# A fused Nystrom attention and feed-forward kernel: smaller first weight chunks, the sums of q of batch 0 on GpSimd, and v loaded in gated pieces

## Chip, cores and metric

The kernel runs on one core of a Trainium2 chip. The metric is the device time of one execution in microseconds (us); of several executions the median is given. The engines are called PE (TensorE's matmuls), DVE (VectorE), ACT (ScalarE), POOL (GpSimd) and SP (SyncE, which only issues DMAs).

## What is computed

Attention by landmarks for 8 batches of 8 heads, 576 tokens and 64 features; then a feed-forward part without nonlinearity. Cut to what matters:

```python
q_lm = q.reshape(B, H, 32, 18, 64).mean(axis=3)        # k_lm likewise
A, Bm, C = sm(q, k_lm), sm(q_lm, k_lm), sm(q_lm, k)    # softmax of scaled products
Z = Bm.T / (norm1(Bm) * norminf(Bm) + 1e-6)
for _ in range(6):
    Z = 2 * Z - Z @ Bm @ Z
x = heads_side_by_side(A @ Z @ C @ v)                  # 4608 x 512
out = (((x @ w1) * (x @ w2)) @ w3) @ w_out             # w1, w2: 512x1024; w3: 1024x1024; w_out: 1024x512
```

## The kernel before

Since nothing stands between w3 and w_out, the kernel first folds them into one 1024x512 matrix (`w34`), once; this is the *fold*. Then it runs batch after batch. For a batch, `attention` (L178) computes landmark scores, the iterated inverse and the small matrices `g` (L403) and `ahat` (L355); the *up* stage (`up`, L422) makes from them, for each of 8 slices of 128 hidden features, two products of 128x576, which ACT copies (`a_sb`, L430) and DVE multiplies (`ab`, L432); the *down* stage (`down`, L439) multiplies `ab` by `w34`, and SP writes the rows out.

**The order is written out by hand.** The schedule is manual: each engine executes its instructions in the order in which the Python code emits them, and a wait at the head of an engine's queue holds all that is behind it. `attention` and `fold` are generators; `steps(g, n)` (L517) runs n pieces of one, and this is how attention of the next batch is woven into the matmuls of the present one. The attention generator has 18 pieces: the landmarks' transposition (L183, first use of `parts`), the small score matrix, two score pieces, and so on, up to four pieces that make `g`.

**The fold** (`fold`, L464). w_out and w3 are float32 and are split into a high and a low float16 term, and a product of two split blocks takes three matmuls (L490): high-high, high-low and low-high. `split(i)` does this for w_out, two row chunks of 128 at a time, both terms on DVE (L469 the high term, L471 the low one). `turn(j, cc)` transposes four 128x128 blocks of w3 on PE (L477); ACT makes their high term (L482) and DVE their low one (L483). `product(j, c)` multiplies them. 64 products are made, in the order of `order` (L499); the dict `before` (L496) says which splits and turns are emitted ahead of which product. Ahead of all this stand 10 matmuls on a zeroed tile (`warm`, L546 to L550), which compute nothing that is used.

**Loads of the fold.** SP loads w3 (first two blocks in halves of 256 KB, L538 to L544), ACT's queue loads w_out in pieces of 512 KB (`load_wout`, L533). GpSimd's queue loads q and k (`load_qk`, L68, float32 in memory to float16) and w1, w2 (`load_weight`, L80). So that these do not crowd the first weights, GpSimd first does a tiny copy from w_out's second piece (`gate`, L552). Two more such gates let w3(4) wait for k of batch 0 (L565) and v of batch 0 for its q (L571).

**The landmarks.** k and q are needed with features on the partitions (`qkT`). For batch 0 PE transposes them (`turn_on_pe`, L94, copies by ACT and DVE, L104), for the others DMA transposes on SP do it (`transposes`, L85, four for a batch in `turn_all`, L512). `landmarks` (L158) sums each 18 tokens: six operations (L166 to L175) for each of k (t=1) and q (t=0), which leave a high and a low term in `parts`. Every such sum is on GpSimd, save that of q of batch 0, which is on DVE (L577), in two halves of 4 heads.

**Around the main loop.** attention of batch 0 runs among the later products of the fold (L581 to L595); in the loop over batches (L600), batch b's up and down stages carry attention of b+1. At the top of batch b SP gets the transposes and the load of v (1152 KB) for b+2 (L604, L605). Behind the up stage GpSimd gets the loads of q and k for b+3 and the landmarks of b+2 (L616 to L619). In the up stage one piece of attention goes into each slice; batch 0 differs (L613: none in the first two, two in the last, and two at a time later in the down stage).

Of the kernel before, what the change touches and what calls it, by code (L numbers as in the profile page):

```python
# [31 lines left out]
def kernel(  # L32
# [46 lines left out]

    def load_weight(t, w):  # L80
# [77 lines left out]
    def landmarks(st, t, eng=nc.gpsimd):  # L158
        if "parts" not in st:
            st["parts"] = pz.tile([128, 2, 2, H, 32], FP16, name="parts")  # L160
        for h0 in ((0,) if eng is nc.gpsimd else (0, 4)):
# [5 lines left out]
            eng.tensor_tensor(out=tr, in0=tr, in1=x[:, :, 2, :], op=ALU.add)  # L167
            t3 = tr.rearrange("p h (l g) -> p h l g", g=3)
# [4 lines left out]

            eng.tensor_copy(out=hi, in_=o)
            eng.tensor_tensor(out=lo, in0=o, in1=hi, op=ALU.subtract)  # L175

# [287 lines left out]
    def fold(pf, wof, w3f, wsp):  # L464
        turned, psW = {}, {}

        def split(i):
            sl = slice(2 * i, 2 * i + 2)
            nc.vector.tensor_scalar(out=wsp[:, 0, sl, :], in0=wof[i], scalar1=WS, scalar2=None,  # L469
                                    op0=ALU.mult)  # L470
            nc.vector.scalar_tensor_tensor(out=wsp[:, 1, sl, :], in0=wof[i], scalar=WS,  # L471
                                           in1=wsp[:, 0, sl, :], op0=ALU.mult, op1=ALU.subtract)
# [13 lines left out]
        def product(j, c):  # L486
# [5 lines left out]
            if c == 7:  # L492
# [3 lines left out]
        before = {0: [(turn, 0, 0), (split, 0), (turn, 1, 0), (split, 1)],  # L496
                  2: [(turn, 0, 1)], 3: [(split, 2)], 6: [(turn, 1, 1)], 7: [(split, 3)],
# [25 lines left out]
    with tc.tile_pool(name="pf", bufs=2) as pf:  # L523
# [3 lines left out]
        def load_w3(j, cc=None):  # L527
            if j not in w3f:
                w3f[j] = pf.tile([128, DF], FP32, name="w3f", bufs=3)
            sl = slice(0, DF) if cc is None else slice(512 * cc, 512 * cc + 512)  # L530
            nc.sync.dma_start(out=w3f[j][:, sl], in_=moe_w3[128 * j:128 * (j + 1), sl])

        def load_wout(i, eng):  # L533
            wof[i] = pf.tile([128, 2, DM], FP32, name="wof", bufs=3)
            eng.dma_start(out=wof[i],
                          in_=moe_w_out[256 * i:256 * i + 256, :].rearrange("(c p) f -> p c f", p=128))
# [3 lines left out]
        load_w3(1, 0)  # L540
        load_wout(1, nc.scalar)
        load_w3(0, 1)
        load_wout(2, nc.scalar)
        load_w3(1, 1)  # L544

# [3 lines left out]
        for _ in range(10):  # L549
            nc.tensor.matmul(psw[:, 0, :], warm[:, 0:128], warm, start=True, stop=True)  # L550

        nc.gpsimd.tensor_copy(out=gate, in_=wof[1][:, 0, 0:1])  # L552
        load_qk(sts[0], 0)
        load_weight(0, moe_w1)
        load_weight(1, moe_w2)
        mask4, par, ones, eye2, iit, onesq, selc, lomask = constants()
        fd = fold(pf, wof, w3f, wsp)
# [102 lines left out]
```

The softmax here doesn't subtract the row's maximum and nothing guards it: scores larger than these inputs give would overflow.

## Time and profile before

| | us |
|---|---|
| median of 8 runs | 296.65 |
| lowest and highest | 294.14, 298.13 |
| the profiled execution | 294.14 |
| its span, first to last instruction | 292.1 |
| PE, DVE, ACT, POOL busy | 274.4, 173.8, 123.7, 141.3 |
| fold with attention of batch 0 (0 to 75.8) | 75.8 |
| batches 0 to 6 of the loop (75.8 to 270.0) | 194.2 |
| batch 7 (270.0 to the end) | 22.1 |

How to read the views: the page's slices cut the span into 40 equal parts of 7.3 us, and a digit is the busy share in tenths; PEclk is the clock granted to TensorE, in the same way. A table by stages gives for stretches of the span the busy time of PE, of its weight loads (PEld), of DVE, ACT and POOL, each with the number of instructions, then the granted clock, the busy share of the DMA engines and the GB/s. A timeline lists instructions in order of time: start, duration, engine, line, operation, what it writes and reads, and in brackets how long the engine was idle before it and what ended that. The chain is what the end is traced back through: start, duration, engine and line. A busy PE is a modelled figure, since matmuls overlap: six matmuls of 512 columns in a row take 1.29 us, one alone shows 0.38.

### The profile page before, as it was taken

How to read it: one execution, taken by the hardware profiler on the slowest of the kernel's cores; microseconds unless marked ns; L12 is line 12 of the kernel's file. 1: busy time of each engine (PE TensorE's matmuls, PEld its weight loads, DVE VectorE, ACT ScalarE, POOL GpSimd, SP SyncE). 2: the span in 40 equal slices, each digit the busy share in tenths (PEclk: the TensorE clock that was granted, in tenths of full speed). 3: DMA queues.
4: the chain of work that ended last, by engine and by line, in shares of the span. 5: the costliest groups of instructions: out<-in, count | busy, mean ns of one | idle time of the engine just before them, and what ended most of it. 6: DMA issues, size and time to landing. Idle time of an engine off the chain costs nothing.

```text
span 292.1 us, 9448 instructions
## 1 busy us (share of the span) xinstructions
PE 274.4 (94%) x4026; PEld 151.1 (52%) x4026; DVE 173.8 (60%) x442; ACT 123.7 (42%) x199; POOL 141.3 (48%) x184
## 2 busy tenths in 40 slices
PE   6899699999999899999999999999999999999993
PEld 3456346443674367436644754375457435744641
DVE  8943743375375676647656766477576656665720
ACT  3134135033471375147426723572466246625531
POOL 1608106295069839923991697069819921500000
PEclk9999889999999999999999999999999999999999
DMA  7999999919948579938996999399968532012124
GB/s 240 288 240 244 236 272 274 170 17 198 196 83 131 145 135 203 214 108 120 183 217 165 159 210 197 90 162 223 207 124 169 119 93 74 2 38 75 37 66 113
DMA packets 61385, 45.56 MB, mean 156 GB/s; under 512 B 34976, under 2 KB 53408, under 8 KB 61344
## 3 DMA queue, kind: packets, MB, share of 16 engines
q1 hardware_dynamic: 46896, 31.86, 48.8%
q0 software_dynamic: 13632, 11.54, 25.2%
q10 hardware_dynamic: 816, 1.57, 1.5%
q8 instruction: 31, 0.51, 0.7%
q14 instruction: 10, 0.08, 0.1%
HBM read 38.80 MB, written 9.44 MB: 165 GB/s over the span
## 4 chain that ended last, share of the span: by engine, by line
PE 80%; DVE 10%; ACT 6%; issue 2%; DVEq 0%; ACTq 0%
PE big L426 18%; PE acc L446 13%; PE acc L490 12%; PE big L446 11%; PE big L412 6%; DVE ab L432 4%; PE big L369 4%; ACT a_sb L430 3%; PE small L305 2%; PE big L477 2%; PE acc L305 2%; PE small L490 2%; PE big L224 2%; PE big L353 1%; PE big L274 1%
## 5 line engine op out<-in xcount | busy, mean ns | idle before, releaser
L426 PE MATMUL big<-ahat,gt 128*128 128x288 f16 x512 | 74.1, 286 | 2.5 <-ACT a_sb L430 1.7
L432 DVE TENSOR_TENSOR ab<-a_sb,big 128x576 f16<-128x576 f16 x64 | 48.0, 750 | 19.6 <-PE big L426 8.4
L426 PEld LDWEIGHTS <-gt 128*128 128x128 f16 x512 | 47.2, 98 | 19.0 <-issue 4.1
L430 ACT CAST a_sb<-big 128x576 f16<-128x576 f32 x64 | 40.9, 639 | 36.7 <-PE big L426 35.9
L235 POOL TENSOR_TENSOR t<-ect 96x384 f32<-96x384 f32 x16 | 15.9, 994 | 78.4 <-ACT ect L228 77.7
L490 PE MATMUL acc<-wsp,w3t 128*128 128x512 f16 x168 | 42.6, 388 | 5.1 <-DVE w3t L483 2.7
L446 PE MATMUL acc<-w,ab 128*128 128x512 f16 (+1 forms) x192 | 41.0, 382 | 0.1
L446 PEld LDWEIGHTS <-ab 128*128 128x128 f16 (+1 forms) x320 | 24.0, 100 | 32.7 <-issue 9.8
L446 PE MATMUL big<-w,ab 128*128 128x512 f16 x128 | 32.8, 381 | 0.3 <-DVE ahat L356 0.3
L490 PEld LDWEIGHTS <-w3t 128*128 128x128 f16 x192 | 18.1, 99 | 25.0 <-issue 5.5
L418 DVE TENSOR_SCALAR gt<-big 128x1024 f16<-128x1024 f32 x16 | 19.6, 1225 | 17.9 <-PE big L412 17.9
L166 POOL TENSOR_TENSOR tr<-qkT 128x768 f32<-128x768 f16 x15 | 24.6, 1641 | 10.8 <-DMA qkT<-qkn 7.1
L452 ACT ACTIVATE o_sb<-acc 128x512 f32<-128x512 f32 x20 | 11.9, 597 | 38.5 <-PE acc L446 37.6
L167 POOL TENSOR_TENSOR tr<-tr,qkT 128x768 f32<-128x768 f32 x15 | 24.6, 1641 | 1.2
L483 DVE SCALAR_TENSOR_TENSOR w3t<-big,w3t 128x512 f16<-128x512 f32 x16 | 11.0, 690 | 16.7 <-ACT w3t L482 16.7
L416 ACT ACTIVATE gt<-big 128x1024 f16<-128x1024 f32 x16 | 16.4, 1023 | 7.9 <-PE big L412 7.9
L482 ACT ACTIVATE w3t<-big 128x512 f16<-128x512 f32 x16 | 9.5, 596 | 23.2 <-PE big L477 18.3
L412 PE MATMUL big<-wup,zt 64*32 64x512 f16 x512 | 19.3, 381 | 0.0
L452 ACT ACTIVATE o_sb<-big 128x512 f32<-128x512 f32 x16 | 9.6, 597 | 21.6 <-PE big L446 21.6
L228 ACT ACTIVATE ect<-big 96x768 f32<-96x768 f32 x16 | 12.9, 806 | 3.3 <-PE big L224 2.9
L356 DVE TENSOR_TENSOR ahat<-eat,big 128x576 f16<-128x576 f16 x16 | 11.9, 749 | 1.2 <-PE big L353 1.2
L172 POOL TENSOR_TENSOR o<-o,tr 128x256 f32<-128x256 f32 x15 | 12.0, 799 | 1.2
(313 smaller groups left out, 354.5 us busy)
## 6 DMA issues: line engine op xcount, KB each, us to landing
vt<-in_v_dram SPq DMA_DIRECT2D x8, 1152.0 KB, 8.9
qkn<-in_k_dram POOLq DMA_DIRECT2D x8, 576.0 KB, 10.1
qkn<-in_q_dram POOLq DMA_DIRECT2D x8, 576.0 KB, 12.4
out_dram<-o_sb SPq DMA_DIRECT2D x24, 192.0 KB, 2.3
w3f<-in_moe_w_dram SPq DMA_DIRECT2D x6, 512.0 KB, 8.2
out_dram<-o_sb SPq DMA_DIRECT2D x24, 128.0 KB, 2.3
wup<-in_moe_w_dram POOLq DMA_DIRECT2D x4, 512.0 KB, 19.4
wof<-in_moe_w_out_dram ACTq DMA_DIRECT2D x3, 512.0 KB, 7.5
```

The lines of the kernel that those rows point to most:

```text
L166: eng.tensor_tensor(out=tr, in0=x[:, :, 0, :], in1=x[:, :, 1, :], op=ALU.add)
L167: eng.tensor_tensor(out=tr, in0=tr, in1=x[:, :, 2, :], op=ALU.add)
L235: nc.gpsimd.tensor_tensor(out=t3[0:NP], in0=e[:, :, 0:3, :], in1=e[:, :, 3:6, :], op=ALU.add)
L412: nc.tensor.matmul(psG[32 * h:32 * h + 32, qd, :], zt[rs, i, h, :], wup[rs, h, w, fs], start=(i == 0), stop=(i == 1), tile_position=(64 * ...
L416: nc.scalar.activation(out=g[:, :, w, fs], in_=psG, func=AXF.Copy, scale=1.0 / ZS)
L418: nc.vector.tensor_scalar(out=g[:, :, w, fs], in0=psG, scalar1=1.0 / ZS, scalar2=None, op0=ALU.mult)
L426: nc.tensor.matmul(p[:, c, 0:HS], st["g"][:, qd, w, 128 * j:128 * j + 128], st["ahat"][qd][:, c, :], start=(qd == 0), stop=(qd == 1))
L430: nc.scalar.copy(out=st["a_sb"], in_=p[:, :, 0:HS])
L432: nc.vector.tensor_tensor(out=st["ab"][:, j, :].rearrange("p (c s) -> p c s", c=2), in0=st["a_sb"], in1=p[:, :, 0:HS], op=ALU.mult)
L446: nc.tensor.matmul(pso[o:o + sz, :], ab[:, j, s0:s0 + sz], w34[:, j, :], start=(j == 0), stop=(j == 7), tile_position=(0, o))
L452: nc.scalar.activation(out=o_sb, in_=pso[:, :], func=AXF.Copy, scale=1.0 / (X64 * X64))
L490: nc.tensor.matmul(psW[j][:, :], turned[j, c // 4][:, a, c % 4, :], wsp[:, b, c, :], start=(c == 0 and a + b == 0), stop=(c == 7 and a == 1))
```

## The change

- w_out is loaded in eight chunks of 128 rows (256 KB) instead of four pieces of two; the first six are shared out between SP's and ACT's queues, beside the first halves of w3, of which one goes to ACT's queue. `split` works on one chunk, with the high term on ACT. The gate of GpSimd's loads is on chunk 4.
- Of the matmuls on zeros 7 stand ahead instead of 10; 3 come behind the first turn and 2 behind the second. The splits and turns are emitted at other products.
- q and k of batch 1 are loaded right behind those of batch 0, ahead of w1 and w2. v of batch 0 and its gate are emitted ahead of the landmarks of k. q of batch 0 is turned after 5 instead of 8 products behind k, and its landmarks are on GpSimd. w3(6) and the DMA transposes of batch 1 are emitted ahead of attention of batch 0, w3(7) with v of batch 1 and the landmarks of batch 1 earlier within it. Ahead of the loop one piece of attention of batch 1 is emitted.
- In the loop, v of b+2 comes in four pieces of two heads at slices 4 to 7 of the up stage. Ahead of each, ACT copies one column of `a_sb` into the piece's place; so the DMA waits for that copy. The landmarks of b+2 are emitted behind slice 5, and q and k of b+3 in four pieces among their operations. Batch 0 gets one piece of attention in each slice, as the others.

```diff
+    def load_v_piece(st, b, i, done):
+        if i == 0:
+            st["vt"] = pin.tile([128, H, 384], FP32, name="vt")
+        hs = slice(2 * i, 2 * i + 2)
+        nc.scalar.copy(out=st["vt"][0:NP, 2 * i, 0:1], in_=done)
+        nc.sync.dma_start(out=st["vt"][0:NP, hs],
+                          in_=v[b, hs].rearrange("h (p r) d -> p h (r d)", p=NP))
+
+    def qk_pieces(st, b):
+        st["qkn"] = pin.tile([128, 2, H, 384], FP16, name="qkn")
+        for t, src in ((1, k), (0, q)):
+            for i in range(2):
+                hs = slice(4 * i, 4 * i + 4)
+                nc.gpsimd.dma_start(out=st["qkn"][0:NP, t, hs, :],
+                                    in_=src[b, hs].rearrange("h (p r) d -> p h (r d)", p=NP))
+                yield
...
-    def landmarks(st, t, eng=nc.gpsimd):
+    def landmarks(st, t, eng=nc.gpsimd, pieces=iter(())):
...
             eng.tensor_tensor(out=tr, in0=tr, in1=x[:, :, 2, :], op=ALU.add)
+            next(pieces, None)
...
             eng.tensor_tensor(out=lo, in0=o, in1=hi, op=ALU.subtract)
+            next(pieces, None)
...
-        def split(i):
-            sl = slice(2 * i, 2 * i + 2)
-            nc.vector.tensor_scalar(out=wsp[:, 0, sl, :], in0=wof[i], scalar1=WS, scalar2=None,
-                                    op0=ALU.mult)
-            nc.vector.scalar_tensor_tensor(out=wsp[:, 1, sl, :], in0=wof[i], scalar=WS,
-                                           in1=wsp[:, 0, sl, :], op0=ALU.mult, op1=ALU.subtract)
+        def split(c):
+            hi, lo = wsp[:, 0, c, :], wsp[:, 1, c, :]
+            nc.scalar.activation(out=hi, in_=wof[c], func=AXF.Copy, scale=WS)
+            nc.vector.scalar_tensor_tensor(out=lo, in0=wof[c], scalar=WS, in1=hi,
+                                           op0=ALU.mult, op1=ALU.subtract)
...
-        before = {0: [(turn, 0, 0), (split, 0), (turn, 1, 0), (split, 1)],
-                  2: [(turn, 0, 1)], 3: [(split, 2)], 6: [(turn, 1, 1)], 7: [(split, 3)],
+        before = {0: [(split, 0), (turn, 0, 0), (warm_up, 3), (split, 1), (turn, 1, 0), (warm_up, 2)],
+                  2: [(split, 2)], 3: [(split, 3)], 5: [(turn, 0, 1)], 6: [(split, 4)],
+                  7: [(split, 5), (turn, 1, 1)], 10: [(split, 6)], 11: [(split, 7)],
                   14: [(turn, 2, 0)]}
...
         load_w3(0, 0)
         load_wout(0, nc.scalar)
-        load_w3(1, 0)
-        load_wout(1, nc.scalar)
+        load_wout(1, nc.sync)
+        load_w3(1, 0, nc.scalar)
+        load_wout(2, nc.sync)
+        load_wout(3, nc.scalar)
         load_w3(0, 1)
-        load_wout(2, nc.scalar)
+        load_wout(4, nc.scalar)
         load_w3(1, 1)
+        load_wout(5, nc.scalar)
...
-        nc.gpsimd.tensor_copy(out=gate, in_=wof[1][:, 0, 0:1])
+        nc.gpsimd.tensor_copy(out=gate, in_=wof[4][:, 0:1])
         load_qk(sts[0], 0)
+        load_qk(sts[1], 1)
         load_weight(0, moe_w1)
...
         load_w3(4)
+        sts[0]["vt"] = pin.tile([128, H, 384], FP32, name="vt")
+        nc.gpsimd.tensor_copy(out=sts[0]["vt"][0:NP, 0, 0:1], in_=sts[0]["qkn"][0:NP, 0, 0, 0:1])
+        load_v(sts[0], 0)
         turn_on_pe(sts[0], 1, 0, nc.scalar.copy)
         turn_on_pe(sts[0], 1, 4, nc.vector.tensor_copy)
         landmarks(sts[0], 1)
-        sts[0]["vt"] = pin.tile([128, H, 384], FP32, name="vt")
-        nc.gpsimd.tensor_copy(out=sts[0]["vt"][0:NP, 0, 0:1], in_=sts[0]["qkn"][0:NP, 0, 0, 0:1])
-        load_v(sts[0], 0)
-        load_qk(sts[1], 1)
-        steps(fd, 8)
+        steps(fd, 5)
         turn_on_pe(sts[0], 0, 0, nc.scalar.copy)
         turn_on_pe(sts[0], 0, 4, nc.vector.tensor_copy)
-        landmarks(sts[0], 0, nc.vector)
-        steps(fd, 3)
+        landmarks(sts[0], 0)
         load_w3(5)
         steps(fd, 4)
+        load_w3(6)
+        turn_all(1)
+        steps(fd, 6)
         at = attention(sts[0])
...
         if b + 2 < B:
             turn_all(b + 2)
-            load_v(sts[b + 2], b + 2)
...
-            steps(at, (0, 0, 1, 1, 1, 1, 1, 2)[j] if b == 0 else 1)
+            steps(at, 1)
+            if b + 2 < B and j > 3:
+                load_v_piece(sts[b + 2], b + 2, j - 4, st["a_sb"][0:NP, 0, 0:1])
             up(st, j, 1)
-        if b + 3 < B:
-            load_qk(sts[b + 3], b + 3)
-        if b + 2 < B:
-            landmarks(sts[b + 2], 1)
-            landmarks(sts[b + 2], 0)
+            if b + 2 < B and j == 5:
+                pieces = qk_pieces(sts[b + 3], b + 3) if b + 3 < B else iter(())
+                landmarks(sts[b + 2], 1, pieces=pieces)
+                landmarks(sts[b + 2], 0, pieces=pieces)
```

## The prediction

> **What bounds the kernel now.** I read the page's busy time and slices first, then stage tables, then the timelines of the stages with idle TensorE.
>
> ```profile
> PE 274.4 (94%) x4026; PEld 151.1 (52%) x4026; DVE 173.8 (60%) x442; ACT 123.7 (42%) x199; POOL 141.3 (48%) x184
> ...
> PE   6899699999999899999999999999999999999993
> ...
> PEclk9999889999999999999999999999999999999999
> ```
>
> PE sets the time: 274.4 of 292.1 us. It is idle for 17.7 us, and it ran slow in the fifth and sixth slice (29 to 44 us). The table by stages says where (first number the stretch's length, second PE's busy time, PEclk near the end):
>
> ```profile
> 32.00:35.00 3.00, 0.27 (x3) 0.05 (x1) 2.72 (x7) 0.00 (x0) 0.00 (x0) 0.97 1.12 246
> 35.00:38.50 3.50, 3.50 (x11) 1.85 (x12) 0.69 (x1) 0.60 (x1) 0.00 (x0) 0.54 1.18 259
> ...
> 75.80:103.40 27.60, 26.18 (x457) 14.67 (x455) 16.94 (x45) 13.24 (x22) 17.82 (x22) 1.00 0.65 128
> ...
> 132.10:158.80 26.70, 26.01 (x458) 14.86 (x457) 17.31 (x46) 13.35 (x22) 17.79 (x22) 1.00 0.98 175
> ...
> 243.50:270.00 26.50, 25.80 (x458) 14.84 (x457) 17.22 (x45) 13.20 (x22) 4.77 (x8) 1.00 0.15 42
> ```
>
> A batch of the main loop leaves PE idle 0.7 us. Batch 6 (243.5), with hardly any DMA or GpSimd work beside it, is only 0.2 us shorter than batch 2 (132.1): nothing done to the loads there can win more than about 0.2 us a batch. The loss is in the fold, and it has two places. The hole at 32 us, in the chain that ended last:
>
> ```profile
> 28.78 0.76 DVE qkT L104
> 29.54 0.47 DVE trv L166
> ...
> 34.00 0.29 DVE parts L175
> 34.30 0.61 DVE w3t L483
> 34.91 0.05 issue
> 34.95 0.61 PE acc L490
> ```
>
> The sums of q (L166 to L175) stand on VectorE ahead of w3t's low term, which PE needs. PE waits 2.73 us, then runs at clock 0.54. The other place is the start, on PE's timeline:
>
> ```profile
> 6.14 0.66 PE L477 MATMUL big<-ident,w3f 128*128 128x128 f32 x4 [0.77 <-DMA w3f<-in_moe_w_dram]
> 7.75 0.38 PE L490 MATMUL acc<-wsp,w3t 128*128 128x512 f16 x1 [0.95 <-DVE wsp L469]
> 9.02 1.24 PE L490 MATMUL acc<-wsp,w3t 128*128 128x512 f16 x5 [0.88 <-DVE wsp L471]
> ```
>
> [...] 0.54 after 2.73 us of idling; 0.95 us did not do it. [...] k and then q of batch 0, issued at 8.95 and 9.90, landed after 9.8 and 11.8 us, in order, with the weights of SP between them. [...]
>
> **The start, part by part.** Removed: VectorE's high terms (0.68 us for two row chunks) and the wait for 512 KB pieces. Added: eight ScalarE high terms, two dummies more in all, and five DMAs on ScalarE's queue instead of three. Before, the first 256 KB of w3 landed 3.5 us after 0.74, at 4.24, beside half of w_out's first piece; w3's second wait ended at 6.14 (about 1 MB moved), the gate on w_out's second piece at 8.81 (about 2 MB). That is 2.67 us per MB, so pairs of 256 KB land at about 4.3, 5.6, 7.0, 8.3, 9.7. ScalarE issues at 0.49 us each; in the compiled order its fifth DMA also waits for w_out chunk 0 (4.3), and the table load (1.28 us in the trace) stands behind it: 4.3 + 0.49 + 1.28 = 6.1. Then ScalarE works every 0.5 us (0.60 each, overlapping, as at 18.93 and 19.43[...]): chunk 0 done at 6.7, w3t 7.2, chunk 1 7.7, w3t 8.2. VectorE is free of the constants at 6.50; its low terms at about 0.65 us (half of 1.23; w3t 0.69) end at 7.35, 7.95, 8.5, 9.1, 9.7, 10.3. At 0.215 us a matmul PE then issues the first four products by 8.2, 8.9, 9.6 and 10.2, and with two more and one turn (0.43) it stands at 11.95. Before, it stood behind the same six and that turn at 13.12, where the next turn started. Gain 1.2 us; nothing if ScalarE came 1.2 later, 1.6 if it needed no wait for chunk 0. The dummies cost nothing: they fill the waits for w3 and for the terms (4.9 to 7.2). Later splits add 0.6 us on a ScalarE that idled 3.3 and 2.4 us between its w3t. So turning k on PE moves from 20.47 to 19.3. It needs k: the gate is now on chunk 4 (8.3 instead of 8.75), so k lands at about 18.4.
>
> **The sums of q.** Removed from VectorE: 12 instructions, 29.46 to 34.2; the hole of 2.73 us goes, and with it the slow clock: 35.35 to 38.50 took 3.15 us for one turn and six matmuls, which cost 0.43 + 1.29 = 1.72 at full clock. PE's way from turning k to the first matmul of attention (L183) was 18.03 us and becomes 18.03 - 2.73 - 1.7 = 13.6 (1.43 in that piece and 0.23 in the matmul before it, 0.61 instead of 0.38): PE would be there at 32.9. Late next is GpSimd, whose sums of k ran 22.60 to 28.75, 6.15 us:
>
> ```profile
> 22.60 1.64 POOL L166 TENSOR_TENSOR tr<-qkT 128x768 f32<-128x768 f16 x1 [3.57 <-DVE qkT L104]
> ...
> 28.08 0.67 POOL L175 TENSOR_TENSOR parts<-o,parts 128x256 f16<-128x256 f32 x1
> 28.70 0.18 POOL L571 CAST vt<-qkn 96x1 f32<-96x1 f16 x1
> ```
>
> Queued on it now: the gate of w3, the gate of v, which moves ahead of the sums and waits for q of batch 0 (9.90 + 11.8 = 21.7 before, about 21.3 now), then both sums: 21.5 + 2 x 6.15 = 33.8. PE waits about 0.9 us there, too short for the clock. L183 comes at 33.8 instead of 38.50: gain 4.7, the start's 1.2 in it (without it PE would come at 34.1, so it adds only 0.3). From below: if q lands 2 us later, 2.7; from above: if GpSimd is early, 38.5 - 32.9 = 5.6.
>
> **What moves with it.** k and q of batch 1 (1.6 us of GpSimd issue) go in front of w1 and w2, and v of batch 0, w3(6) and batch 1's transposes go earlier. w1 and w2 had landed by 13.0 + 22.5 = 35.5; with 1.15 MB more of writes in front, some 10 us later, and they are first used at 64.20 before, 59.5 now. v took 12.5 us from 28.91; from 21.8 it is there at 34.3, and is needed at 49.99 - 4.7. w3(5), behind it, at about 36, needed at 40.4; it had landed after 13.9 from 29.3. On SP the four transposes now stand ahead of w3(7) and batch 1's v: they took 43.58 to some 56 before, and started at about 29 they hold w3(7) to about 43, with its first turn at 65.42 - 4.7 = 60.7. All this costs nothing, by those covers; uncovered, each us late is a us. The sums for batch 1 started at 56.60 on a DMA wait of 7.1 us; now after the transposes, in the forties, well before batch 1's L183 at about 71.
>
> **The main loop.** Batch 0 now takes attention's steps evenly, like batch 2: 131.65 to 158.32 is 26.67 us from L183 to L183; before, 75.81 to 102.99 was 27.18. Gain 0.5. The gates of v are 4 tiny ScalarE copies in each of 6 batches; [...] the trace's nearest row ScalarE's 128x128 at 277. Behind each is the next a_sb (L430), for which VectorE's products wait. In that part of batch 2 ScalarE idled 0.98, 1.29 and 0.93 us before a_sb: I take 0; the upper end is 24 x 0.28 = 6.7, the lower a gain of 0.2 x 6 = 1.2. SP waits at those gates, and the output DMAs stand behind them, but they come only after the last product. GpSimd issues four qk pieces instead of two, between the old 1.6 us and four times 0.8 (I take 2.6), but its sums for batch 4 ended at 154.87 for L183 at 158.32: a cover of 3.4.
>
> **Sum.** 4.7 + 0.5 = 5.2 us. The profiled execution took 294.14 (span 292.1 and 2.0 around it): 288.9. That is the lowest of eight; the median is 2.5 above. I forecast the median: 296.65 - 5.2 = 291.4; by itself 290 to 293.
>
> **Rivals.** (a) Half comes: q of batch 0 lands 2 us later, 293.4. For: the DMA share is near 1 in that stretch. Against: SP's weights in that time are the same 1.5 MB. (b) More comes: GpSimd is never late and the loop gains 1.2: 296.65 - 5.6 - 0.5 - 1.2 = 289.4. (c) Slower: the GpSimd queue. v's gate holds both sums until q has landed; each us of it moves L183, and once PE has waited some 2.7 us the slow clock costs 1.7 more. Level with before at q landing at 21.3 + 5.2 - 1.7 = 24.8; at 27, 296.65 + 2.2 = 298.9. For: q is in the most crowded stretch. Against: before, it landed at 21.7. (d) The ScalarE gates all lie on the path: 296.65 - 5.2 + 6.7 = 298.1; against, the idle times above.
>
> **Numbers.** Forecast 0.52, (a) 0.19, (b) 0.16, (c) 0.05, (d) 0.03, and 0.05 that several small delays leave it within a measurement of before. Range 288.8 to 295.2: below it lies a part of (b), above it the last three. A measurement tells about 0.5% (1.5 us): faster 0.87, same 0.05, slower 0.08.
>
> **What would show it.** Right: no DVE trv rows, PEclk full at 29 to 44, L183 at about 34 with PE waiting about 0.9 us behind GpSimd's parts, first steady products near 8, batches 1 to 6 unchanged, 26.7 for batch 0. Wrong: a PE gap over 2 us near 33, w3 or v as a releaser, or a_sb waits in batches 0 to 5.

## The result, and the profile after

The changed kernel takes 289.62 us in the median (288.09 to 292.61), the kernel before beside it 296.75 (294.14 to 299.95): ratio 0.9787, 95% interval 0.9753 to 0.9821, which is 6.3 us of 296.75; the medians differ by 7.1. Profile against profile, 294.14 stands against 289.62, 4.5 us. The forecast took 5.2 us off both, which gives 291.4 for the median and 288.9 for the profiled execution. Here and below a ratio leaves out executions that are over 1.5% slower than the fastest of their kernel; a median does not.

The page of the changed kernel, TensorE's busy time, its slices and its granted clock:

```profile
PE 273.8 (95%) x4028; PEld 150.7 (52%) x4028; DVE 167.3 (58%) x430; ACT 131.7 (46%) x231; POOL 152.3 (53%) x200
...
PE   7999999989999999999999999999999999999994
...
PEclk9999999999999999999999999999999999999999
```

PE does the same work (273.8 for 274.4 us) in a shorter span: it idles 13.9 us instead of 17.7, and the fifth and sixth slices have the full clock. DVE gave work up, ACT and POOL took it. A new digit 8 stands in the ninth slice, at 58 to 65 us; more of that below. The table by stages of the changed kernel (columns as before):

```profile
32.00:35.00 3.00, 2.54 (x14) 1.16 (x13) 0.69 (x1) 0.60 (x1) 2.32 (x4) 1.00 1.12 199
35.00:38.50 3.50, 3.25 (x24) 1.59 (x23) 2.20 (x6) 1.89 (x4) 0.00 (x0) 1.00 1.10 275
72.60:99.20 26.60, 25.95 (x458) 14.80 (x456) 17.04 (x44) 14.03 (x26) 18.92 (x24) 1.00 0.62 123
...
128.20:154.90 26.70, 26.01 (x458) 14.85 (x457) 17.41 (x45) 14.06 (x26) 18.92 (x24) 1.00 0.84 167
239.00:265.50 26.50, 25.80 (x457) 14.71 (x454) 17.27 (x45) 13.35 (x22) 4.77 (x8) 1.00 0.15 43
```

Between 32 and 35 us PE is busy 2.54 us instead of 0.27, and GpSimd stands where VectorE stood. Batch 0 (third row) now has nearly the length and idle time (0.65 us) of batch 2 (fourth row, 0.69). The chain that ended last shows what took the place of VectorE's sums:

```profile
22.08 0.18 POOL vt L594
22.26 1.61 POOL tr L183
...
28.41 1.61 POOL tr L183
...
33.87 0.68 POOL parts L192
34.55 0.04 issue
34.60 0.38 PE small L201
```

L183 to L192 are now the lines of `landmarks`, and L201 the transposition that was L183. The wait of v's gate ended at 22.08, when q had landed (22.03); both sums follow without a pause, and PE takes the last of them at 34.60. So the chain in this stage is q's transfer and then GpSimd. The start, on PE's timeline:

```profile
4.68 0.80 PE L494 MATMUL big<-ident,w3f 128*128 128x128 f32 x4 [0.32 <-DMA w3f<-in_moe_w_dram]
5.32 0.81 PE L572 MATMUL big<-warm 128*128 128x512 f16 x3
5.97 0.60 PE L494 MATMUL big<-ident,w3f 128*128 128x128 f32 x4
6.40 0.59 PE L572 MATMUL big<-warm 128*128 128x512 f16 x2
7.40 0.61 PE L507 MATMUL acc<-wsp,w3t 128*128 128x512 f16 x2 [0.40 <-ACT w3t L499]
8.24 1.19 PE L507 MATMUL acc<-wsp,w3t 128*128 128x512 f16 x4 [0.23 <-DVE w3t L500]
```

The gaps of 0.77, 0.95 and 0.88 us are now 0.32, 0.40 and 0.23. Put together, between marks that both profiles have (the end of the fold is its last product; the loop is cut at L183, now L201, of attention of batches 2, 3, 4 and 5):

| stretch | before | after | difference |
|---|---|---|---|
| to the turning of k on PE | 20.47 | 19.64 | -0.83 |
| from there to the second matmul of L183/L201, batch 0 | 18.25 | 14.96 | -3.29 |
| from there to the end of the fold | 36.72 | 37.97 | +1.25 |
| batch 0 | 27.55 | 26.62 | -0.93 |
| batch 1 | 28.66 | 29.01 | +0.35 |
| batch 2 | 26.67 | 26.67 | 0 |
| batch 3 | 29.21 | 28.66 | -0.55 |
| the rest | 104.57 | 104.17 | -0.40 |
| span | 292.1 | 287.7 | -4.4 |

The +0.35 and the -0.55 of batches 1 and 3 are not counted as effects of the change. Without an edit to these batches, batch 1 took 28.66 us in experiment 6 and 28.65 in experiment 8, and batch 3 took 29.01 in experiment 8.

One row clearly goes the wrong way: 1.25 us were lost again in the fold. PE's timeline there:

```profile
62.46 0.40 PE L430 MATMUL big<-wup,zt 64*32 64x512 f16 x6
63.74 0.61 PE L430 MATMUL big<-wup,zt 64*32 64x512 f16 x10 [0.88 <-issue]
64.28 1.47 PE L507 MATMUL acc<-wsp,w3t 128*128 128x512 f16 x6
```

A group of 16 like matmuls (one product of `wup` and `zt`) stops behind its sixth. Elsewhere such a group takes 0.56 us from its start to the next instruction's; here 64.28 - 62.46 = 1.82, which is 1.26 more. The profile shows nothing that PE waited for, and within one group there is no operand that could be late. The last section returns to it.

### The profile page after: what moved, and what is told of

Read it like the earlier page. It is cut to its first block, busy times and chain, and to the rows that moved or that the text cites. A ratio compares the mean times of both kernels' runs of the same rounds, so it can differ in the third digit from the quotient of the medians.

```text
span 287.7 us, 9554 instructions
## 1 busy us (share of the span) xinstructions
PE 273.8 (95%) x4028; PEld 150.7 (52%) x4028; DVE 167.3 (58%) x430; ACT 131.7 (46%) x231; POOL 152.3 (53%) x200
## 3 DMA queue, kind: packets, MB, share of 16 engines
q10 hardware_dynamic: 720, 1.31, 1.3%
## 4 chain that ended last, share of the span: by engine, by line
PE 77%; ACT 7%; DVE 6%; POOL 4%; issue 3%; DMA 1%; ACTq 0%; DVEq 0%; POOLq 0%
PE big L444 18%; PE acc L464 13%; PE big L464 11%; PE acc L507 9%; PE big L430 6%; DVE ab L450 5%; PE big L387 4%; ACT a_sb L448 3%; PE small L323 2%; PE acc L323 2%; PE big L371 2%; PE big L242 1%; ACT lm L206 1%; PE big L494 1%; PE small L507 1%
## 5 line engine op out<-in xcount | busy, mean ns | idle before, releaser
L507 PE MATMUL acc<-wsp,w3t 128*128 128x512 f16 x168 | 41.6, 380 | 1.4 <-ACT w L510 0.7
L436 DVE TENSOR_SCALAR gt<-big 128x1024 f16<-128x1024 f32 x16 | 19.6, 1225 | 19.3 <-PE big L430 19.3
L183 POOL TENSOR_TENSOR tr<-qkT 128x768 f32<-128x768 f16 x16 | 26.3, 1645 | 7.2 <-DMA qkT<-qkn 7.1
L470 ACT ACTIVATE o_sb<-acc 128x512 f32<-128x512 f32 x20 | 11.9, 597 | 34.3 <-PE acc L464 34.3
L184 POOL TENSOR_TENSOR tr<-tr,qkT 128x768 f32<-128x768 f32 x16 | 26.2, 1641 | 1.3
L190 POOL TENSOR_TENSOR o<-o,tr 128x256 f32<-128x256 f32 x16 | 13.0, 812 | 1.3
```

Source lines behind the costliest of these rows:

```text
L183: eng.tensor_tensor(out=tr, in0=x[:, :, 0, :], in1=x[:, :, 1, :], op=ALU.add)
L436: nc.vector.tensor_scalar(out=g[:, :, w, fs], in0=psG, scalar1=1.0 / ZS, scalar2=None, op0=ALU.mult)
L470: nc.scalar.activation(out=o_sb, in_=pso[:, :], func=AXF.Copy, scale=1.0 / (X64 * X64))
L507: nc.tensor.matmul(psW[j][:, :], turned[j, c // 4][:, a, c % 4, :], wsp[:, b, c, :], start=(c == 0 and a + b == 0), stop=(c == 7 and a == 1))
```

## Experiments

The theory at the outset was the prediction's: what counts is VectorE's sums, with the slow clock behind them; the even steps give 0.5; start and loop give little. The rival was that the unforecast gain comes from the start.

**1. The sums of q alone.** The kernel before with one edit:

```diff
-        landmarks(sts[0], 0, nc.vector)
+        landmarks(sts[0], 0)
```

> The kernel before with one edit: the sums of q of batch 0 on GpSimd, nothing moved for it. Theory (the hole and its slow clock are the gain, and GpSimd's queue sets where attention starts): on GpSimd these sums stand behind v's gate and the issue of q and k of batch 1, so they run from about 30.5 to 36.7; PE comes to the first matmul of attention at 20.47 + 13.6 = 34.1 and waits 2.6 us, close to the wait that halved the clock. Attention starts at 36.7 instead of 38.7: 2.0 us faster than before, or only 0.3 to 0.6 if the clock drops there too. Rival (moving the sums is the whole gain of the fold): PE never waits, 4 us or more faster. Rival (the loop's loads are the gain): within 0.5 us of before in the median.

Measured: 294.78 us, ratio 0.994 (0.9918 to 0.9963), 1.8 us faster. This edit alone leaves v's gate and the issue of batch 1's q and k between the two sums, so GpSimd did those of q from 32.87 to 39.0. PE's timeline shows the new wait:

```profile
38.33 0.38 PE L183 MATMUL small<-parts,iit 128*128 128x512 f16 x1 [1.73 <-POOL parts L174]
39.08 0.38 PE L183 MATMUL small<-parts,iit 128*128 128x512 f16 x1 [0.37 <-POOL parts L175]
```

VectorE's hole is gone, but PE now waits for GpSimd. Moving the sums is worth some 2 us by itself. That the rest of the fold's gain needs q earlier on PE and GpSimd's queue in the new order is a reading of this wait of 1.73 us. (All of this profile is some 2.4 us late from the start on; experiment 5 says why.)

**2. The slow clock alone.** The kernel before, with matmuls on zeros, which compute nothing that is used, filling the hole:

```diff
...
+            if n == 28:
+                dummies(12)
             product(j, c)
...
```

> The kernel before with 12 matmuls on zeros put ahead of product 28, in the hole of 2.73 us: VectorE's sums and the wait stay, only TensorE is kept busy (12 x 0.215 = 2.6 us). Theory (1.7 us of the loss is clock): the granted clock stays at 1.0 from 29 to 44, one turn and six matmuls take 1.7 us instead of 3.15, and the kernel is 1.7 us faster. If the median of before lies 2.6 us over its profiled execution because the clock drops for longer in other executions, more than 1.7. Rival (the clock is not set by this hole): no change, within 0.5 us, or slower by what the dummies delay.

Measured: 294.80, ratio 0.9945 (0.9919 to 0.9971), 1.6 us faster. The clock is full in all 40 slices, and the turn and six matmuls behind the hole take 0.44 + 1.29 us, as the prediction had worked out (1.72). The hole's 2.7 us were still spent. L183 began at 36.92 instead of 38.50, so of the 4.7 us forecast for the fold some 1.6 was the clock. The span of this profile, 292.1, is none the shorter: among other things PE stopped for 0.82 us at 55.84 and for 0.66 at 206.15, in the way of the stop at 63.74.

**3. The old start in the changed kernel.** Pieces, splits, gate, dummies and the order of the first turns as before:

```diff
-        before = {0: [(split, 0), (turn, 0, 0), (warm_up, 3), (split, 1), (turn, 1, 0), (warm_up, 2)],
+        before = {0: [(turn, 0, 0), (split, 0), (turn, 1, 0), (split, 1)],
...
-        warm_up(7)
+        warm_up(10)
...
```

> The changed kernel with the start of before: w_out in pieces of two row chunks on ScalarE's queue, both split terms on VectorE, ten matmuls on zeros ahead and none later, the gate on the second piece. Theory (GpSimd sets the start of attention, so the start's gain is mostly covered): k is turned at 20.5 instead of 19.6, but attention starts 0.3 to 0.5 us later than in the changed kernel, because sums of k start when k has been turned and copied, at 22.6 instead of 22.2: the time is 0.3 to 0.5 us over the changed kernel. Rival (the start's gain counts whole): 0.8 to 1.2 us over the changed kernel.

Measured: 290.05, ratio 0.9791 (0.9758 to 0.9825): behind the changed kernel by 0.4 us in the median and 0.1 by the ratio, which these runs can't tell from nothing. In its profile PE turned k at 20.47, 0.83 later than in the changed kernel, and took the second sum at 34.94, where the two profiles of the changed kernel have 34.60 and 34.31 (experiment 9). So 0.3 to 0.6 us of the start's gain is left there, for 0.3 forecast; GpSimd covers the rest.

**4. The old loop in the changed kernel.**

```diff
...
+            load_v(sts[b + 2], b + 2)
...
-            if b + 2 < B and j > 3:
-                load_v_piece(sts[b + 2], b + 2, j - 4, st["a_sb"][0:NP, 0, 0:1])
...
-            if b + 2 < B and j == 5:
-                pieces = qk_pieces(sts[b + 3], b + 3) if b + 3 < B else iter(())
-                landmarks(sts[b + 2], 1, pieces=pieces)
-                landmarks(sts[b + 2], 0, pieces=pieces)
+        if b + 3 < B:
+            load_qk(sts[b + 3], b + 3)
+        if b + 2 < B:
+            landmarks(sts[b + 2], 1)
+            landmarks(sts[b + 2], 0)
```

> The changed kernel with the loads of the loop as before: v of b+2 in one piece behind the transposes, q and k of b+3 and the landmarks behind the up stage; no copies on ScalarE; batch 0 keeps one piece of attention in each slice. Theory (no engine on the path waits for these loads): the time is that of the changed kernel within 0.4 us. Rival (spread loads are what makes the median gain 6 us where the profiles differ by 4.5): 1.5 us or more slower than the changed kernel. Rival (ScalarE's copies cost): faster than the changed kernel by up to 2 us.

Measured: ratio 0.9791 (0.975 to 0.9831), five executions at 288.98 to 291.76. The profiled one was disturbed as a whole (876 us) and is left out, so the kernel was run again:

> The changed kernel with the old loop of attention's batches (v loaded in one piece behind the batch's gate, q and k at the end of the batch, landmarks there), as run before without a profile that can be read. Both ends are from that run: 289.7, the changed kernel's time within 0.4%. Theory (loads of the loop are worth nothing): batches 2 and 4 take 26.7 us and 1 and 3 take 28.7 to 29.2, as in both kernels, and PE's waits on ScalarE's a_sb and lm are those of the changed kernel, near 1.7 us each. Rival (the new loop costs or gains in one batch what the other gives back): one of the batches 1 to 4 differs by over 0.4 us from that of the changed kernel.

Measured: 291.52, ratio 0.9838 (0.9796 to 0.988). In its profile batches 0 to 2 took 26.61, 29.16 and 26.66 us (26.62, 29.01, 26.67 in the changed kernel), and PE's waits on a_sb and lm were 1.6 and 1.7. Batch 3 took 29.69 for 28.66; 0.68 of that is a gap of the kind seen at 63.74, again inside a group of 16. So the rival's mark is met in one batch, and mostly by something other than the loads. Together the two runs put what the new loop wins between nothing and some 2 us. Neither run of the old loop is faster than the changed kernel beyond the noise, so no cost of the new one shows; that it wins something isn't shown.

**5. Dummies in the gaps of the start.** The changed kernel with all ten dummies ahead and none in the gaps:

```diff
-        before = {0: [(split, 0), (turn, 0, 0), (warm_up, 3), (split, 1), (turn, 1, 0), (warm_up, 2)],
+        before = {0: [(split, 0), (turn, 0, 0), (warm_up, 0), (split, 1), (turn, 1, 0), (warm_up, 0)],
...
-        warm_up(7)
+        warm_up(10)
```

> The changed kernel with its ten matmuls on zeros all ahead, as before, and none in the gaps of the first turns. The runs of the kernel before show two levels of mean clock, 0.990 to 0.992 (295 us) and 0.981 to 0.987 (296 to 300 us), while the changed kernel mostly has 1.0. Theory (the gaps of the start halve the clock in a part of the executions, and the dummies in them prevent it): the mean clock falls to about 0.994 in more than half of the executions, and those take about 1 to 1.7 us more; the median rises by about 1. Rival (the smaller chunks close the gaps, the dummies do nothing): clock and time stay as in the changed kernel, within 0.4 us.

Measured: 289.11, ratio 0.9756 (0.9722 to 0.9789), clock full in all slices. The rival was right: with the smaller chunks the dummies do nothing. The start's gaps on PE's timeline are now two:

```profile
7.38 0.61 PE L507 MATMUL acc<-wsp,w3t 128*128 128x512 f16 x2 [1.19 <-ACT w3t L499]
8.22 0.97 PE L507 MATMUL acc<-wsp,w3t 128*128 128x512 f16 x3 [0.23 <-DVE w3t L500]
```

The first is longer than any of the three in the profile of before (0.77, 0.95 and 0.88), but together they are 1.42 us and not 2.60. And the other way round, the kernel before with three dummies in each of its first gaps:

```diff
-        before = {0: [(turn, 0, 0), (split, 0), (turn, 1, 0), (split, 1)],
+        before = {0: [(turn, 0, 0), (dummies, 3), (split, 0), (turn, 1, 0), (dummies, 3), (split, 1)],
...
```

> The kernel before with three matmuls on zeros behind each of the first two turns; nothing else. Theory (the start's slow clock is what puts the median of before some 2 us over its profiled execution): the clock is at 0.990 to 0.992 in nearly all executions, since only the hole at 32 us is left, and the median falls by about 1.5 us, towards 295. Rival (the scatter of before has another cause, such as the loads): the clock keeps its two levels, the median stays within 0.5 us.

Measured: 294.37, ratio 0.9932 (0.9905 to 0.9959), 2.0 us faster, and the mean granted clock 0.991 to 0.996 in all 13 executions. The kernel before has two levels: of the 33 executions beside experiments 1 to 4, 12 had a clock of 0.990 to 0.992 and took 294.7 to 295.5 us, the other 21 0.981 to 0.987 and 295.8 to 299.7; of the 18 beside experiments 5 to 7, 4 were on the upper level. What the lower level is, the profile of experiment 1 shows: it has the old start, and its clock fell there. The clock in its slices:

```profile
PEclk9799999999999999999999999999999999999999
```

The gaps of its start on PE's timeline, and three stretches of its table, with the clock as the third number from the end:

```profile
8.51 0.38 PE L490 MATMUL acc<-wsp,w3t 128*128 128x512 f16 x1 [1.30 <-DVE wsp L469]
9.76 1.96 PE L490 MATMUL acc<-wsp,w3t 128*128 128x512 f16 x5 [0.88 <-DVE wsp L471]
```

```profile
6.72:10.14 3.42, 1.24 (x7) 0.63 (x7) 2.94 (x4) 1.01 (x2) 1.26 (x2) 1.00 0.86 322
10.14:13.55 3.41, 3.41 (x11) 1.78 (x10) 2.54 (x4) 0.60 (x1) 3.41 (x6) 0.50 0.79 265
13.55:16.96 3.41, 3.41 (x19) 1.84 (x18) 2.35 (x4) 0.60 (x1) 0.45 (x1) 1.00 1.23 222
```

PE idled 2.18 of the 3.42 us up to 10.14, and the clock was halved for the 3.41 us that follow; k was turned at 22.9 instead of 20.47. The profiled execution of before (294.14) did not have it; by their clock, most of its others did. This is the part of the gain that a comparison of the two profiles cannot show. The last section has an estimate of why the same program has two levels.

**6. The sums of q back on VectorE, in the changed kernel.**

```diff
-        landmarks(sts[0], 0)
+        landmarks(sts[0], 0, nc.vector)
```

> The changed kernel with the sums of q of batch 0 back on VectorE, the moved loads, gates, turns and dummies kept. Theory (the sums on VectorE hold w3t's low term, wherever they stand): VectorE is held from about 26.5 to 31.3, now ahead of the low term of turn (3,0), which PE needs after two matmuls; PE waits about 5.5 us from 26.3 and then runs slow for some 3 us more: attention starts at 39 to 41, and the time is 5 to 7 us over the changed kernel, so about that of before. Rival (the moved loads and the earlier schedule are the gain, not the sums): at most 2 us over the changed kernel.

Measured: 292.13, ratio 0.9848 (0.9803 to 0.9892): behind the changed kernel by 2.5 us in the median and 1.8 by the ratio, and the intervals of the two ratios just meet. That is too little for the theory (5 to 7) and near the rival's mark (at most 2). PE's timeline shows the wait again:

```profile
32.51 4.67 PE L507 MATMUL acc<-wsp,w3t 128*128 128x512 f16 x13 [3.30 <-DVE w3t L500]
```

The wait is that of the old hole, and L201 begins at 38.74, as before the change (38.50). But the fold ends at 75.51, only 2.94 later than in the changed kernel: the gap in the group of 16, 1.26 us, is not in this kernel. So part of what the moved sums win at L201, the changed kernel loses again at 63.74. Without the moved sums this kernel still wins 4.5 us over the kernel before (by the ratio): 0.9 in batch 0 (26.62 here too), and the larger part not in the profiles, whose spans differ by 1.8. That fits the clock of the start (see 5), but no run takes it apart further.

**7. v's gate behind the sums of k.** The wait at GpSimd's gate (2.67 us before 22.08) seemed to be idle time ahead of both sums:

```diff
-        sts[0]["vt"] = pin.tile([128, H, 384], FP32, name="vt")
-        nc.gpsimd.tensor_copy(out=sts[0]["vt"][0:NP, 0, 0:1], in_=sts[0]["qkn"][0:NP, 0, 0, 0:1])
-        load_v(sts[0], 0)
         turn_on_pe(sts[0], 1, 0, nc.scalar.copy)
         turn_on_pe(sts[0], 1, 4, nc.vector.tensor_copy)
         landmarks(sts[0], 1)
+        sts[0]["vt"] = pin.tile([128, H, 384], FP32, name="vt")
+        nc.gpsimd.tensor_copy(out=sts[0]["vt"][0:NP, 0, 0:1], in_=sts[0]["qkn"][0:NP, 0, 0, 0:1])
+        load_v(sts[0], 0)
```

> The changed kernel with v's gate and load moved behind the sums of k, so that GpSimd does not wait for q of batch 0 first. In the changed kernel's trace the gate ended at 22.2 and k's copies at 21.5, and PE waited 0.37 us twice at the first matmuls of attention. Theory (GpSimd's queue sets that point, by half a us at most): sums of k start at 21.5, attention starts 0.5 to 0.7 us earlier, the time falls by 0.4 to 0.6 us; v is there at about 41, needed at 45. Rival (another load is then late): the cv products or a turn of w3 wait, and the time rises.

Measured: 295.93 in the median, some 6 us slower than the changed kernel. Five executions took 295.1 to 297.1 us with a mean clock of 0.986 or 0.987, and one took 291.11 with 0.998. My theory fell. L201 came at 34.29, hardly earlier than in the changed kernel (34.60, and 34.31 in experiment 9), and PE's timeline then has a wait for w3, and later a stop inside a group of like matmuls:

```profile
44.30 1.11 PE L494 MATMUL big<-ident,w3f 128*128 128x128 f32 x4 [3.43 <-DMA w3f<-in_moe_w_dram]
...
59.90 0.40 PE L387 MATMUL big<-sz__780,tz__778 32*32 32x96 f32 x15 [1.56 <-issue]
```

The slices:

```profile
PEclk9999997979999999999999999999999999999999
```

SyncE's queue says why. Its timeline in the changed kernel:

```profile
22.29 0.33 SPq L77 DMA_DIRECT2D vt<-in_v_dram  x1
22.71 1.35 SPq L549 DMA_DIRECT2D w3f<-in_moe_w_dram  x1
```

And in this one:

```profile
28.16 0.33 SPq L77 DMA_DIRECT2D vt<-in_v_dram  x1
28.59 0.96 SPq L549 DMA_DIRECT2D w3f<-in_moe_w_dram  x2
```

w3's part 5 stands behind v on the queue. v waits for its gate, so part 5 waits too: issued at 28.6 instead of 22.71, it landed at 44.3 instead of 39.6, and its turn on PE stood at 41.01 in the changed kernel. A wait of 3.43 us follows, and the slow clock after it, between 0.7 and 0.8 in the mean of its slice. The second dip of the clock stands behind the stop of 1.56 us. That 291.11 is an execution without the slow clock fits its mean of 0.998; it has no profile.

**8. The same with w3's part 5 ahead of v.** Tile, gate and load of v are taken from their old place, as in 7:

```diff
...
-        steps(fd, 5)
+        steps(fd, 1)
+        load_w3(5)
+        sts[0]["vt"] = pin.tile([128, H, 384], FP32, name="vt")
+        nc.gpsimd.tensor_copy(out=sts[0]["vt"][0:NP, 0, 0:1], in_=sts[0]["qkn"][0:NP, 0, 0, 0:1])
+        load_v(sts[0], 0)
+        steps(fd, 4)
...
-        load_w3(5)
```

> The changed kernel with v's gate and load behind the sums of q's partner k on GpSimd, as in the earlier run with the late gate, but with the load of w3's part 5 put ahead of v on SyncE's queue, so that it no longer stands behind v. Theory (what cost the late gate 6 us was only w3's part 5, which landed at 44.3, behind v on the queue, and the slow clock that followed the wait): w3's part 5 lands before 38, the turn that waited 3.43 us no longer waits, the first matmul of attention's batch 0 keeps its earlier start at 33.7 to 34.1, and the time is 0.3 to 0.6 us under that of the changed kernel, 289.0 to 289.5, ratio 0.975 to 0.979. Rival (v itself is then late, issued near 28 and there near 43, or the next part of w3 takes the wait over): a wait of PE of 2 us or more between 40 and 48, and a time of 292 or more.

Measured: 287.7 (287.48 to 288.46), ratio 0.9724 (0.9695 to 0.9753): the fastest of all. Part 5, issued behind part 4 and landed at 28, is no longer waited for, and the 6 us are gone: v's place ahead of part 5 was what cost them. The gain over the changed kernel is 1.9 us, more than the 0.3 to 0.6 I expected, and it hardly comes from where I looked. L201 took its second sum at 34.22, for 34.60 and 34.31 in the two profiles of the changed kernel, which is 0.1 to 0.4 us. The rest is the stop inside the group of 16 (1.26 us in the one, 1.54 in the other), which PE's timeline does not have here:

```profile
61.91 0.62 PE L430 MATMUL big<-wup,zt 64*32 64x512 f16 x16
62.47 1.47 PE L507 MATMUL acc<-wsp,w3t 128*128 128x512 f16 x6
```

Its margin is thin: v is issued at 28.09, lands 17.0 us later, at 45.1, and is first used at 45.49.

**9. The changed kernel again, as the measure for 8 and 10.**

> The changed kernel itself, unaltered, on the same chip as the other three, to compare with them directly: 288 to 291, ratio 0.976 to 0.981. If the granted clock of its executions has one level (0.994 to 1.0) where that of the kernel before has two, the theory that the start's clock makes part of the gain stands; if it shows executions at 0.98 to 0.99 too, that theory is too simple.

Measured: 289.6 (289.07 to 292.23), ratio 0.9795 (0.9758 to 0.9832). Five executions had a clock of 0.997 to 1.0, one 0.993 (292.23): nearly one level, but not wholly.

**10. The uneven steps of batch 0 in the changed kernel.**

```diff
-    steps(at)
...
-            steps(at, 1)
+            steps(at, (0, 0, 1, 1, 1, 1, 1, 2)[j] if b == 0 else 1)
...
-            steps(at, 2 if n == 6 and nd == 8 else 1)
+            steps(at, 2 if n == 6 and nd == 8 or b == 0 and n > 3 else 1)
```

> The changed kernel with one part undone: attention's batch 0 takes its fold steps in the old, uneven numbers again. Theory (the even steps are worth what batch 0 differs by in the two profiles, 26.62 for 27.18 at the first, 0.5 us): the stretch from the first matmul of batch 0's turn to batch 1's is longer by 0.4 to 0.6, the time 0.5 over that of the changed kernel, 290.1, ratio 0.979 to 0.981. Rival (the steps move work within the batch only): the two stretches of batches 0 and 1 together come out the same within 0.15, and so does the time. Both are near what the measurement can tell; the stretches in the profile decide.

Measured: 289.82, ratio 0.9785 (0.9742 to 0.9829), which does not tell it from experiment 9. The stretches do: batch 0 takes 27.55 us and batch 1 28.66, both as before the change, where the changed kernel has 26.62 and 29.01. So the even steps win 0.93 us in batch 0. The 0.35 of batch 1 isn't theirs: experiments 6 and 8 have the even steps too, and batch 1 took 28.66 and 28.65 us there, while in experiment 8 batch 3 took 29.01. In the changed kernel it arises in one place, at 106.11, ahead of a matmul of the up stage.

## Why the prediction was right, and where it was not

The place of the loss, the two causes of the hole and the order in which things would wait were foreseen. That the number came so near owes something to luck. 289.62 lies in the stated range but under the 290 to 293 that the forecast gave for itself. In the profiles, 4.4 us of span were won: the fold gave 2.9 at its end and not 4.7, batch 0 gave 0.93 and not 0.5, and the rest scattered. Some 2 us more, which no step had, came from the start's clock (experiment 5); 4.4 and 2.0 are 6.4, beside 6.3 measured by the ratio.

**The fold: right, with two sizes off.** The forecast was a gain of 4.7 at L183; the profiles show 4.1 (38.72 to 34.60, by the matmul that needs the last sum). q had landed at 22.0 and not 21.3, so GpSimd, whose sums took 12.3 us as forecast, ended at 34.54 and not 33.8. The step "PE would be there at 32.9" failed by 0.95: PE stood at L201 at 33.85, because k was turned at 19.64 (forecast 19.3) and the way from there took 14.2 us instead of 13.6. Hence PE waited only 0.37 us behind GpSimd, and not 0.9. That the slow clock behind the hole cost some 1.6 to 1.7 us, experiment 2 confirms.

**The start: the mechanism was right, its worth was not.** ACT's table load began at 4.94 (forecast 4.8), the first split ended at 6.86 (6.7), the first products ran at 7.40 and 8.24; the gain at the turning of k was 0.83 instead of 1.2, of which 0.3 to 0.6 remained at L201 and no more than 0.4 in the time (experiment 3); 0.3 was worked out. But I forecast the median by the sum of one profile, and that profile was one of the third or less without the start's slow clock. Experiment 5 prices this at 2.0 us in the kernel before. It is the term that was missing: with it, 5.2 becomes about 7. "0.95 us did not do it" was read from one gap of one execution; two gaps of one window, together 2.18 us, were followed by the slow clock in experiment 1 (last section), and by their clock two thirds of the executions of before lost it in the start. The new start and, in part, the new wait for GpSimd remove it: with the old start in the changed kernel (experiment 3) four of six executions had a clock of 0.994 and took 290.05 to 290.94, two had 1.0 and took 289.4 to 289.6, so there it costs about 1 us and not 2. That GpSimd's sums hide the other half is my reading, not shown by a run.

**What was said to move with it: the covers held, the times did not.** w3's part 5 landed at 39.6, not 36, for a turn at 41.0: a margin of 1.4 us where I counted 4.4. v came at 37.0 for 34.3. w1 and w2 came at 49.2, 13.7 later than before instead of 10, and were first used at 60.1. The four transposes of batch 1 held SyncE's queue for 23.4 us and not 12, so w3's part 7 went out at 52.33 (43 forecast), and batch 1's sums began at 52.45 instead of in the forties, still 20 us ahead of use. Experiment 7 shows what lay behind such a cover: 6 us, as soon as part 5 lost 4.7.

**A loss that no step had:** the 1.26 us at 63.74. It is the whole of the difference between the fold's gain at L201 and at its end.

**The loop: right but for one size.** The even steps gave 0.93 and not 0.5 (experiment 10). The 0.5 was misread: "from L183 to L183" it took 27.18 us from 75.81 on, but PE's timeline of before has no L183 there, and the loop's first matmul starts at 75.44:

```profile
75.44 2.88 PE L426 MATMUL big<-ahat,gt 128*128 128x288 f16 x20
78.15 0.59 PE L183 MATMUL small<-parts,iit 128*128 128x512 f16 x2
```

From 75.44, where the loop begins (and not at 75.8), batch 0 took 27.55, which is 0.88 over the 26.67 of batch 2. As forecast, there was nothing for the loads and ScalarE's gates within what experiment 4 can tell (each of the 24 gates took 0.19 us in the trace); PE's waits on a_sb were 1.7 us in all eight batches together, before and after. Rival (d), 6.7 us, is excluded by this, rival (c) by q at 22.0. Of the signs named, the missing VectorE rows, the full clock and L183 at about 34 came; the wait of 0.9 did not. Rival (b)'s 289.4 lies nearest the median, but not for its reason: GpSimd was late, and the loop's gain was not what made it.

## What to carry to other kernels

A load that waits for a gate held the next load on its queue, which cost 6 us in experiment 7: before a gate is moved, list what stands behind it and when each is needed. A profile is one execution; where the mean granted clock has levels from execution to execution, find out on which one the profile stands before a sum made in it is set against a median. Several gaps near each other are to be added up before they are called short: in experiment 1 1.30 and 0.88 us made 2.18, and the slow clock followed. And where several causes guard the same point in time, undoing one of them gives back only the distance to the next: parts don't add up.

## What the runs showed of the hardware

**Idle time within a window of 3.41 us.** The traces keep the times at which the granted clock changed. Within one execution they lie 3.41 us or a multiple of it apart (at 4.08, 34.80, 38.21 and 290.80 in the profile of before, at 5.05 and 288.36 in that of the changed kernel); the first, to full speed, comes at a different time in each, from 4.08 to 6.89 us. Cut each profile into windows on its own grid, and leave out those in which PE has nothing left to do. Then PE idled over 2 us in five windows: 2.18 in the start of experiment 1, 2.57 in the hole of before, 2.44 in that of experiment 5's second kernel, 2.94 in experiment 6 and 3.19 in experiment 7. Each was followed by one window at half the clock (the mean granted clock of these executions is 0.992 to 0.994, and 0.987 in experiment 7, where a second window was slow). Of three windows with 1.56 to 1.75 us one was so followed (1.56, experiment 7), and none with less; the starts of before and of experiments 2 and 3 had 1.47, 1.56 and 1.51 at most. That gaps which fall into one window count together, and that the place of the windows decides, is my reading of these windows, not tested by a run of its own. An estimate from the profiles: wherever a window is laid, the fullest of the start of before holds 1.31 to 2.38 us of idle time; in the changed kernel it is at most 0.73, and 1.42 without the dummies. That would give the kernel before two levels and the changed kernel one, as measured but for three executions at 0.991 to 0.994.

**PE's stops ended behind packets of an instruction queue.** In the table of queues of the changed kernel:

```profile
q8 instruction: 31, 0.51, 0.8%
```

31 packets of 16 KB; PE executes 8056 matmuls and weight loads, 260 for each packet. Whose instructions they hold, the profile does not say. In the profiles of this case, but for the disturbed one, PE stopped 11 times for 0.58 to 1.56 us with no wait for another engine or a DMA in the profile. Ahead of these stops stand 961, 1217 or 1218, 4801 to 4803 or 5825 of PE's instructions (1217 in the changed kernel: 1200 matmuls and weight loads, 16 semaphore instructions and a drain), numbers that lie 256 or a multiple of it apart, to within two; and each stop ended 1.3 to 1.7 us after a packet of this queue had landed. In the changed kernel such a packet moved from 61.2 to 62.3, and PE, stopped in mid-group, went on at 63.74. In experiment 9 it moved at 61.1 to 62.5, and PE went on at 63.74 too, though it had come 0.27 us earlier; in experiment 8 it moved at 58.8 to 60.1, and PE, at that place at 62.1, did not stop. That these stops are waits for PE's program is my reading of these counts and times, not shown by a run. What makes a packet late is open: in both profiles of the changed kernel, w3's part 7 and v of batch 1, 1664 KB, issued from 52.3 to 53.4, were landing until 61.9 and 63.5, but in experiment 8 they landed until 61.2. No run isolates either.

**VectorE beside GpSimd.** In experiment 6 VectorE's first half of the sums ran while GpSimd did those of k, the second half after. Its two additions and the first of the next step on VectorE's timeline:

```profile
26.24 0.90 DVE L183 TENSOR_TENSOR trv<-qkT 128x384 f32<-128x384 f16 x1
27.18 0.64 DVE L184 TENSOR_TENSOR trv<-trv,qkT 128x384 f32<-128x384 f32 x1
27.85 0.68 DVE L189 TENSOR_TENSOR o3v<-trv 128x128 f32<-128x128 f32 x1
...
29.40 0.55 DVE L183 TENSOR_TENSOR trv<-qkT 128x384 f32<-128x384 f16 x1
29.98 0.56 DVE L184 TENSOR_TENSOR trv<-trv,qkT 128x384 f32<-128x384 f32 x1
30.57 0.33 DVE L189 TENSOR_TENSOR o3v<-trv 128x128 f32<-128x128 f32 x1
```

GpSimd's sums of k ended at 28.34. Beside them VectorE's three took 0.35, 0.08 and 0.35 us longer than in the second half. In the profile of before GpSimd's sums had ended (28.75) when VectorE's began (29.46), and both halves took 0.55, 0.56 and 0.33. Why VectorE was slower, no run shows.
